# Parking the second experts' weights as plain values, and splitting them where they are used

## The chip, the cores and the metric

The kernel runs on one core of one Trainium2 chip. The metric is the device time of one execution in microseconds. The core's engines work side by side, each through its own instructions in order: TensorE (PE, with its weight loads as PEld), VectorE (DVE), ScalarE (ACT), GpSimd (POOL) and SyncE (SP), which here issues every DMA transfer.

## The reference

Three layers follow one another on 2304 tokens (4 batches of 576) and a model width of 512. All is float32; the expert weights arrive as float64.

```python
scores = scale * q @ k.T          # 4 batches, 8 heads, 576 x 576, head width 64
attn   = softmax(where(block_i >= block_j, scores, -1e9))   # blocks of 64
x  = (attn @ v)                   # heads joined: 2304 x 512
h  = max(x @ w1, x @ w2, x @ w3)  # first experts, width 768
x2 = h @ w_out                    # 2304 x 512
g  = 1 / (1 + exp(-(x2 @ w_gate)))  # second experts, width 1536
out = (g * (x2 @ w_val)) @ w_out2 # 2304 x 512
```

## The kernel before

**Arithmetic.** TensorE gets every float32 operand as two float32r parts: the high part is the value rounded by a copy (ScalarE or VectorE), the low part is the value less the high part (a subtraction on VectorE or GpSimd). A product is three matmuls: high by high, high by low, low by high. So each weight must be split once for each copy of it in SBUF.

**First stage, to about 551 us.** Attention for 32 jobs (batch, pair of heads, early or late rows) and the first experts for eight chunks of 256 or 320 tokens run interleaved. The work is a list of `Op`s with an engine (B means VectorE or ScalarE), a cost, dependencies, an earliest and a latest time and, for some, a ring of buffers. `plan()` is a list scheduler over these: it gives each engine's order, which TensorE, VectorE, ScalarE and SyncE then follow as written (`run_plan`). GpSimd's place is found by the framework's scheduler. The results x2 go out to DRAM (`x2d`).

In the same stretch the second experts' weights are parked in DRAM. The two halves of each of 12 block matrices (`park_pair`, from plan time 112 on, one every 20) are loaded as float64 words (`take`), turned into float32 in place (`first_part` on ScalarE, `shift` and `join` on VectorE), and combined into seven blocks of 128 x 256: three of the four quarters and four sums (a Strassen-Winograd scheme with seven products). `split_ops` splits each block: a high copy on VectorE or ScalarE, a low subtraction on GpSimd, and a store (L768) of both parts. The `sp` ring through which all this goes has two buffers. `park_out` does the same with the 12 output matrices, in two halves each. That makes 84 + 24 = 108 blocks.

**Second stage, from 551 us.** The tokens go in three chunks of 768. `take_x` loads a chunk of x2 and forms the seven combinations XC (four differences `t`, seven high copies on ScalarE, seven low subtractions on VectorE; L1062, L1066, L95). For each of 12 pairs `first`, `middle` and `last` run seven products of six matmuls of 384 columns (L1108 to L1110); VectorE adds their banks (L1121), ScalarE takes the sigmoid (L1133), VectorE multiplies (L1138), ScalarE and GpSimd split the hidden value (L1147, L95). The order of the products is first(n), last(n-1), middle(n). Then 12 x 6 output units (L1157 to L1159) use the output matrices. `take_w` loads one pair's seven split blocks, 1792 KB, into one of three buffers; `take_o` loads one split output matrix into one of four. In this stage only TensorE's order is written out; the framework's scheduler orders the other engines by the times given to `on` and its own estimate of when things are ready.

The stage's buffers lie where those of the first stage lay, so a write there waits for the last reader of the old tile. TensorE accumulates into eight banks, three to a pair.

Of the kernel before, what the change touches and what calls it, by code (L numbers as in the profile page):

```python
# [67 lines left out]
RING = {"qk": 2, "v": 3, "s": 3, "t": 2, "o": 1, "m": 2, "w": 8, "raw": 4, "tmp": 4, "st": 3, "sp": 2}  # L68
# [3 lines left out]
def block_attention_moe_moe(ctx: ExitStack, tc, k1, q1, v1, k2, q2, vt, wa, wb, out):  # L72
# [33 lines left out]
    sp_p = one.enter_context(tc.tile_pool(name="sp", bufs=RING["sp"]))  # L106
# [3 lines left out]
    pairs_d = [dram.tile([128, 7, 512], F32, name=f"pairs{n}") for n in range(NF2)]  # L110
    outs_d = [dram.tile([128, 2, PC], F32, name=f"outs{f}") for f in range(NF2)]
# [548 lines left out]
    def build():  # L660
# [57 lines left out]
        sums = []  # L718

        def word_ops(i, t):  # L720
# [17 lines left out]

            def join():
                lo, hi, _ = words()  # L740
                V.scalar_tensor_tensor(
                    out=hi, in0=hi, scalar=3, in1=lo, op0=ALU.logical_shift_left, op1=ALU.bitwise_or
                )

            ld = Op("S", 0.1, take, list(sums), ring="raw", size=512e3)
            new, last = [ld], [ld]
            if wide:
                p = Op(*act(PC), first_part, [ld])
                s = Op("V", 0.36, shift, [ld])
                last = [Op(*vec(PC), join, [p, s])]  # L750
                new += [p, s] + last
# [3 lines left out]
            return ld, last, lambda: words()[2] if wide else f32(box["x"])  # L755

        def split_ops(n, x, deps, dest, t):
            box = {}

            def high(e):  # L760
                box["t"] = sp_p.tile([128, 512], F32R, tag="sp", name="sp")[:, : 2 * n]
                copy(e, box["t"][:, :n], x())

            def low():
                sub("G", box["t"][:, n:], x(), f32(box["t"][:, :n]))

            def put():
                nc.sync.dma_start(out=dest, in_=f32(box["t"]))  # L768

            h = Op(*both(n, False), high, deps, ring="sp")  # L770
            l = Op("G", 0.2 + 0.0025 * n, low, [h])
            d = Op("S", 0.1, put, [l], size=1024 * n)
            h.frees = [d]
            for o in (h, l, d):
                o.early, o.late = t, t + P["slack"]
            return l

        def park_pair(n):
# [3 lines left out]
            la, da, xa = word_ops(3 * f + c, t)  # L782
            lb, db, xb = word_ops(3 * f + 3 + c, t)
# [508 lines left out]
```

## Time and profile before

| what | value |
|---|---|
| three timed runs | 980.91, 981.3, 984.16 us (median 981.3) |
| the profiled execution | 978.59 us, of which the span of the trace is 975.5 us |
| busy in the span | PE 910.8 us, DVE 596.8, ACT 418.7, POOL 166.4 |
| DMA | 146.80 MB read, 37.75 MB written |
| mean granted TensorE clock | 0.976 |

Busy time is read per engine: an engine that is busy for 93% of the span leaves 7% to be won by better feeding, unless its own work shrinks. A granted clock of 1.00 is 2.4 GHz, 0.50 is 1.2 GHz; a mean between them is a mixture. Idle time of an engine that nobody waits for costs nothing.

### The profile page before, as it was taken

How to read it: one execution, taken by the hardware profiler on the slowest of the kernel's cores; microseconds unless marked ns; L12 is line 12 of the kernel's file. 1: busy time of each engine (PE TensorE's matmuls, PEld its weight loads, DVE VectorE, ACT ScalarE, POOL GpSimd, SP SyncE). 2: the span in 40 equal slices, each digit the busy share in tenths (PEclk: the TensorE clock that was granted, in tenths of full speed). 3: DMA queues.
4: the chain of work that ended last, by engine and by line, in shares of the span. 5: the costliest groups of instructions: out<-in, count | busy, mean ns of one | idle time of the engine just before them, and what ended most of it. 6: DMA issues, size and time to landing. Idle time of an engine off the chain costs nothing.

```text
span 975.5 us, 15409 instructions
## 1 busy us (share of the span) xinstructions
PE 910.8 (93%) x5696; PEld 838.0 (86%) x5696; DVE 596.8 (61%) x1393; ACT 418.7 (43%) x1004; POOL 166.4 (17%) x186
## 2 busy tenths in 40 slices
PE   5598988998989999899999899999999999999998
PEld 4587988887878888789999899988899988999986
DVE  7999676878978959778842555570155550355500
ACT  6975443557655747467621323340133320333300
POOL 0000022212223222121200013230032320123300
PEclk9797999999999999999999999999999999999999
DMA  9911355655565664666335357775467663577233
GB/s 308 364 55 49 115 165 195 192 182 167 188 204 188 215 192 151 205 208 196 108 115 227 131 198 249 274 259 195 166 236 267 252 237 130 192 259 261 76 130 108
DMA packets 64763, 185.55 MB, mean 190 GB/s; under 512 B 8624, under 2 KB 25008, under 8 KB 60080
## 3 DMA queue, kind: packets, MB, share of 16 engines
q1 hardware_dynamic: 64688, 184.58, 55.3%
q8 instruction: 44, 0.72, 0.3%
q14 instruction: 31, 0.25, 0.1%
HBM read 146.80 MB, written 37.75 MB: 189 GB/s over the span
## 4 chain that ended last, share of the span: by engine, by line
PE 52%; DMA 4%; DVE 4%; issue 3%; POOL 1%; ACT 0%; SPq 0%; DVEq 0%; POOLq 0%; ACTq 0%
PE acc L1108 8%; PE acc L1109 8%; PE acc L1110 8%; PE acc L1157 5%; PE acc L1159 5%; PE acc L1158 5%; PE ps_m L527 2%; PE ps_m L525 2%; PE ps_m L526 2%; DMA pairs<-sp 2%; DVE xc L95 1%; PE ps_o L492 1%; PE ps_m L563 1%; PE ps_m L565 1%; PE ps_m L564 1%
## 5 line engine op out<-in xcount | busy, mean ns | idle before, releaser
L525 PE MATMUL ps_m<-XT,w 128*128 128x256 f32 (+1 forms) x576 | 179.4, 311 | 9.0 <-DVE m L536 3.7
L527 PE MATMUL ps_m<-XT,w 128*128 128x256 f32 (+1 forms) x576 | 173.4, 301 | 3.9 <-DVE w L95 3.9
L1108 PE MATMUL acc<-xc,wg 128*128 128x384 f32 x504 | 170.1, 338 | 4.3 <-DVE u L1121 2.9
L526 PE MATMUL ps_m<-XT,w 128*128 128x256 f32 (+1 forms) x576 | 173.2, 301 | 0.0
L1109 PE MATMUL acc<-xc,wg 128*128 128x384 f32 x504 | 169.5, 336 | 1.3 <-DVE xc L95 1.3
L1110 PE MATMUL acc<-xc,wg 128*128 128x384 f32 x504 | 169.6, 336 | 0.0
L525 PEld LDWEIGHTS ps_m<-XT,w 128*128 128x128 f32 x576 | 112.0, 194 | 13.7 <-DVE m L536 4.4
L527 PEld LDWEIGHTS ps_m<-XT,w 128*128 128x128 f32 x576 | 111.8, 194 | 4.5 <-DVE w L95 4.5
L526 PEld LDWEIGHTS ps_m<-XT,w 128*128 128x128 f32 x576 | 112.1, 195 | 0.7
L1108 PEld LDWEIGHTS acc<-xc,wg 128*128 128x128 f32 x504 | 95.4, 189 | 6.4 <-DVE u L1121 4.1
L95 POOL TENSOR_TENSOR sp<-praw,sp 128x256 fp32r<-128x256 f32 x60 | 49.0, 824 | 289.3 <-ACT sp L86 225.1
L1109 PEld LDWEIGHTS acc<-xc,wg 128*128 128x128 f32 x504 | 95.5, 189 | 1.7 <-DVE xc L95 1.6
L1110 PEld LDWEIGHTS acc<-xc,wg 128*128 128x128 f32 x504 | 95.3, 189 | 0.0
L400 ACT ACTIVATE E<-ps_s,nm 128x256 f32<-128x256 f32 (+3 forms) x128 | 66.4, 524 | 44.1 <-DVE nm L395 43.7
L1159 PE MATMUL acc<-ow,hid 128*128 128x512 f32 x216 | 84.2, 390 | 0.0
L1158 PE MATMUL acc<-ow,hid 128*128 128x512 f32 x216 | 84.1, 390 | 0.0
L1157 PE MATMUL acc<-ow,hid 128*128 128x512 f32 x216 | 84.0, 389 | 0.0
L90 DVE COPY osb<-acc 128x512 f32<-128x512 f32 x6 | 4.1, 692 | 118.5 <-PE acc L1159 110.8
L1121 DVE TENSOR_TENSOR u<-acc,p 128x384 f32<-128x384 f32 x72 | 40.1, 557 | 49.4 <-PE acc L1110 44.4
L1121 DVE TENSOR_TENSOR u<-acc,u 128x384 f32<-128x384 f32 x72 | 40.1, 556 | 46.3 <-PE acc L1110 45.1
L95 POOL TENSOR_TENSOR hid<-c,hid 128x384 fp32r<-128x384 f32 x18 | 19.1, 1061 | 286.8 <-ACT hid L1147 286.8
L492 PE MATMUL ps_o<-PT,v 128*64 128x320 f32 (+3 forms) x448 | 56.3, 377 | 10.4 <-DMA v<-in_v_dram 9.5
(109 smaller groups left out, 1815.4 us busy)
## 6 DMA issues: line engine op xcount, KB each, us to landing
wg<-pairs SPq DMA_DIRECT2D x36, 1792.0 KB, 7.4
pairs<-sp SPq DMA_DIRECT2D x84, 256.0 KB, 2.3
praw<-in_wb_dram SPq DMA_DIRECT2D x36, 512.0 KB, 4.5
ow<-outs SPq DMA_DIRECT2D x36, 512.0 KB, 3.3
qk<-in_k_dram SPq DMA_DIRECT2D x16, 576.0 KB, 4.3
wland<-in_wa_dram SPq DMA_DIRECT2D x5, 1536.0 KB, 17.4
outs<-sp SPq DMA_DIRECT2D x24, 256.0 KB, 2.5
v<-in_vt_dram SPq DMA_DIRECT2D x16, 320.0 KB, 3.4
```

Of the source, the lines that this page charges most:

```text
L95: (V if e == "V" else G).tensor_tensor(out=out, in0=a, in1=b, op=ALU.subtract)
L400: A.activation(E[h][:, e : e + 128 * (t + 1)], j.s[h, t], AF.Exp, bias=j.nm[:, c : c + 1], scale=1.0, accum_out=j.sm[:, c : c + 1],)
L525: T.matmul(ps, wt[:, 0, w, k], xh[:, k], start=(k == 0), stop=False)
L526: T.matmul(ps, wt[:, 0, w, k], xl[:, k], start=False, stop=False)
L527: T.matmul(ps, wt[:, 1, w, k], xh[:, k], start=False, stop=(k == KD - 1))
L1108: T.matmul(ps, w[:, 0, h], x[:, 0, h], start=start and h == 0, stop=False, skip_group_check=True)
L1109: T.matmul(ps, w[:, 0, h], x[:, 1, h], start=False, stop=False, skip_group_check=True)
L1110: T.matmul(ps, w[:, 1, h], x[:, 0, h], start=False, stop=h == 1, skip_group_check=True)
L1121: V.tensor_tensor(out=o, in0=BK[c, n, b][:, :N2], in1=x, op=ALU.add)
L1157: T.matmul(ps, h[:, 0, ct], w[:, 0], start=(f == 0), stop=False)
L1158: T.matmul(ps, h[:, 0, ct], w[:, 1], start=False, stop=False)
L1159: T.matmul(ps, h[:, 1, ct], w[:, 0], start=False, stop=(f == NF2 - 1))
```

## The change

The blocks and sums are parked as float32 values, unsplit. `join` writes its result into a new tile in block order (`blocks`, or `outw` for an output matrix) in place of the loaded words, so that a loaded tile comes free at once; the sums are formed from there, and four stores per pair and one per output matrix take the whole to DRAM (`put`), 60 in all in place of 108. `split_ops` and its `sp` ring are gone. The `raw` ring keeps its four buffers and now also carries `blocks` and `outw`; the ring of v goes from three to four.

In the second stage each pair's weights come as three parts: x (three blocks, used by `first`), z (two, `middle`) and y (two, `last`). For each part and chunk `take_w` loads the values into one of four `wr` buffers, copies the high part on ScalarE and subtracts the low part on VectorE (x, y) or GpSimd (z), into one of two buffers for each part. `take_o` does so with an output matrix (ScalarE and VectorE). The seven combinations, the temporaries and the other tiles of the stage are placed over other tiles of the first stage: the temporaries and XC[0] over the `raw` ring, the other six over the first three buffers of `w`. A sigmoid on a small tile is issued at TB - 24 on the plan's clock.

```diff
-RING = {"qk": 2, "v": 3, "s": 3, "t": 2, "o": 1, "m": 2, "w": 8, "raw": 4, "tmp": 4, "st": 3, "sp": 2}
+RING = {"qk": 2, "v": 4, "s": 3, "t": 2, "o": 1, "m": 2, "w": 8, "raw": 4, "tmp": 4, "st": 3}
...
-    sp_p = one.enter_context(tc.tile_pool(name="sp", bufs=RING["sp"]))
...
-    pairs_d = [dram.tile([128, 7, 512], F32, name=f"pairs{n}") for n in range(NF2)]
-    outs_d = [dram.tile([128, 2, PC], F32, name=f"outs{f}") for f in range(NF2)]
+    pairs_d = [dram.tile([128, 7, 256], F32, name=f"pairs{n}") for n in range(NF2)]
+    outs_d = [dram.tile([128, PC], F32, name=f"outs{f}") for f in range(NF2)]
...
-        def word_ops(i, t):
+        def word_ops(i, t, ring, dest, dring=None):
...
+            def two(x):
+                return x.rearrange("p (a n) -> p a n", a=2)
+
             def join():
+                o = dest()
+                if not wide:
+                    V.tensor_copy(o, two(f32(box["x"])))
+                    return
                 lo, hi, _ = words()
                 V.scalar_tensor_tensor(
+                    out=o.bitcast(U32), in0=two(hi), scalar=3, in1=two(lo),
+                    op0=ALU.logical_shift_left, op1=ALU.bitwise_or,
...
+            ld = Op("S", 0.1, take, ring, ring="raw", size=512e3)
...
+            j = Op("V", 0.72, join, deps, ring=dring)
+            new.append(j)
...
+            ld.frees = [j]
...
+        def put(out, src, deps, t):
+            d = Op("S", 0.1, lambda: nc.sync.dma_start(out=out, in_=src()), deps, size=512e3)
+            d.early, d.late = t, t + P["slack"]
+            return d
+
+        order_ = []
...
+            def corner(k):
+                def g():
+                    if "d" not in box:
+                        box["d"] = raw_p.tile([128, 4, 256], F32, tag="raw", name="blocks")
+                    return box["d"][:, ::3] if k == 0 else box["d"][:, 1:3]
+                return g
...
+            la, ja = word_ops(3 * f + c, t, list(order_), corner(0), "raw")
+            lb, jb = word_ops(3 * f + 3 + c, t, [la], corner(1))
+            order_[:] = [jb]
+            p = lambda f_, k: lambda: f_(k)
+            o1 = Op(*vec(256), two_of(ALU.add, p(s, 0), p(d, 1), p(d, 2)), [jb], ring="raw")
+            o2 = Op(*vec(256), two_of(ALU.subtract, p(s, 1), p(s, 0), p(d, 0)), [o1, ja])
+            o3 = Op(*vec(256), two_of(ALU.subtract, p(s, 2), p(d, 0), p(d, 1)), [o1, ja])
+            o4 = Op(*vec(256), two_of(ALU.subtract, p(d, 1), p(d, 3), p(s, 1)), [o2, o3])
...
+            order_[:] = [o1]
+            g = pairs_d[n]
+            w = [
+                put(g[:, 1:3], lambda: box["s"][:, 0:2], [o2], t),
+                put(g[:, 6], lambda: box["s"][:, 2], [o3], t),
+                put(g[:, 0], lambda: box["d"][:, 0], [ja], t),
+                put(g[:, 3:6], lambda: box["d"][:, 1:4], [o4], t),
+            ]
+            o1.frees = w[:2] + [o4]
+            ja.frees = w[2:]
...
+                box["d"] = raw_p.tile([128, PC], F32, tag="raw", name="outw")
+                return box["d"].rearrange("p (a n) -> p a n", a=2)
...
+            ld, j = word_ops(3 * f + 2, t, list(order_), dest, "raw")
+            order_[:] = [j]
+            j.frees = [put(outs_d[f], lambda: box["d"], [j], t)]
...
-    hid_p = pool("hid", 1)
-    xc_p = pool("xc", 1)
+    HID = []
+
+    def hidden(n):
+        p = pool(f"hid{len(HID)}", 1)
+        HID.extend(p.tile([128, 2, HC], F32R, name=f"hid{len(HID) + k}") for k in range(n))
+
+    XC = {}
+
+    def combos(ks):
+        p = pool(f"xc{len(XC)}", 1)
+        for k in ks:
+            XC[k] = p.tile([128, 2, 2, N2], F32R, name=f"xc{k}")
+
+    hidden(3)
+    ost_p = pool("ost", 3)
     tt_p = pool("tt", 2)
+    combos((0,))
+    hidden(2)
+    combos((4, 5, 1, 3, 2, 6))
     pt_p = pool("pt", 15)
-    hie_p = pool("hie", 1)
-    ost_p = pool("ost", 3)
+    hidden(7)
     ow_p = pool("ow", 4)
-    wg_p = pool("wg", 3)
+    wg_p = pool("wg", 2)
+    wr_p = pool("wr", 4)
     xr_p = pool("xr", 1)
+    warm = pool("warm", 1).tile([128, 8], F32, name="warm")
...
+    def take_w(c, n, part, t):
+        k0, k1, low = {"x": (0, 3, "V"), "y": (3, 5, "V"), "z": (5, 7, "G")}[part]
+        box = {}
+
+        def get():
+            box["r"] = wr_p.tile([128, 3, 256], F32, tag="wr", name="wr")[:, : k1 - k0]
+            nc.sync.dma_start(out=box["r"], in_=pairs_d[n][:, k0:k1])
+
+        def high():
+            WG[c, n, part] = wg_p.tile([128, 2, k1 - k0, 256], F32R, tag="wg" + part, name="wg" + part)
+            A.copy(WG[c, n, part][:, 0], box["r"])
+
+        def rest():
+            w = WG[c, n, part]
+            sub(low, w[:, 1], box["r"], f32(w[:, 0]))
+
+        on(t - 5.0, get)
+        on(t, high)
+        on(t + 0.7, rest)
...
+        def high():
             OW[c, f] = ow_p.tile([128, 2, PC], F32R, tag="ow", name="ow")
-            nc.sync.dma_start(out=f32(OW[c, f]), in_=outs_d[f])
-        on(t, g)
+            A.copy(OW[c, f][:, 0], box["r"])
+
...
+            part, i = (("x", 0), ("z", 0), ("y", 0), ("y", 1), ("x", 1), ("x", 2), ("z", 1))[k]
+            w = WG[c, n, part][:, :, i].rearrange("p s (k c) -> p s k c", k=2)
...
-    free_w = [TB - 22.0, TB - 15.0, TB - 8.0]
+    first_w = {"x": (18.0, 8.0), "y": (14.0, 4.0), "z": (16.0, 6.0)}
+
+    def next_w(c, n, part, t):
+        g = NF2 * c + n + 2
+        if g < NF2 * (TOK // HC):
+            take_w(g // NF2, g % NF2, part, t)
+
+    on(TB - 25.0, lambda: V.memset(warm, 0.0))
+    on(TB - 24.0, lambda: A.activation(warm, warm, AF.Sigmoid))
+    for n in range(2):
+        for part in "xzy":
+            take_w(0, n, part, TB - first_w[part][n])
     for c in range(TOK // HC):
...
-            take_w(c, n, free_w.pop(0))
...
+            next_w(c, n, "x", t)
...
+            next_w(c, n, "z", t)
...
+            next_w(c, n, "y", t)
...
-            if f >= 4:
-                take_o(c, f, t)
...
+            if f + 4 < NF2:
+                take_o(c, f + 4, t)
```

## Rows read from the trace of the kernel before

**Rows 1.** Windows: busy us (instructions) of PE, PEld, DVE, ACT, POOL; clock; DMA.

```profile
25.00:75.00 50.00, 38.21 (x268) 34.22 (x266) 47.95 (x125) 40.88 (x98) 0.00 (x0) 0.84 0.59 200
115.00:400.00 285.00, 258.97 (x1908) 234.29 (x1908) 229.19 (x606) 163.86 (x431) 67.41 (x84) 0.98 0.57 185
141.00:148.00 7.00, 6.13 (x36) 5.44 (x37) 6.29 (x17) 4.17 (x13) 0.51 (x2) 0.76 0.58 199
400.00:500.00 100.00, 98.67 (x693) 90.54 (x692) 82.38 (x212) 63.52 (x155) 18.67 (x24) 0.99 0.48 154
504.00:551.00 47.00, 47.00 (x321) 47.00 (x322) 13.73 (x27) 7.35 (x15) 0.00 (x0) 1.00 0.45 169
551.00:568.00 17.00, 12.63 (x54) 11.22 (x53) 12.14 (x17) 6.35 (x10) 0.00 (x0) 0.80 0.66 230
699.00:772.00 73.00, 73.00 (x423) 73.00 (x422) 37.65 (x68) 23.73 (x49) 19.16 (x18) 1.00 0.66 244
```

**Rows 2.** Who VectorE waited for, 115 to 500 us: total, times, longest.

```profile
DVE sp L90 <- DMA pairs<-sp: 27.0, 13, 5.6
```

**Rows 3.** The same for ScalarE, 115 to 500 us.

```profile
ACT sp L86 <- DMA pairs<-sp: 27.3, 17, 6.1
```

**Rows 4.** Timeline: VectorE's stalled casts and TensorE's gaps, first and last of nine.

```profile
139.54 0.71 DVE L90 CAST sp<-sums 128x256 fp32r<-128x256 f32 x1 [2.23 <-DMA pairs<-sp]
141.08 0.39 PE L563 MATMUL ps_m<-HR,w 128*128 128x256 f32 x1 [2.16 <-ACT HR L547]
...
395.63 0.29 DVE L90 CAST sp<-sums 128x256 fp32r<-128x256 f32 x1 [3.20 <-DMA pairs<-sp]
398.86 0.58 PE L378 MATMUL ps_s<-K,Q 128*128 128x512 f32 x1 [2.24 <-ACT E L436]
```

**Rows 5.** The tile sp: its high copies (ns min/median/max).

```profile
L86 ACT CAST sp<-praw x43: 413/424/442, 123.4 to 482.3; 128x256 fp32r<-128x256 f32 x43
L90 DVE CAST sp<-sums x28: 277/294/823, 135.8 to 396.3; 128x256 fp32r<-128x256 f32 x28
L90 DVE CAST sp<-praw x17: 277/291/667, 173.3 to 489.3; 128x256 fp32r<-128x256 f32 x17
```

**Rows 6.** Timeline of TensorE near the start of the kernel.

```profile
38.60 1.55 PE L492 MATMUL ps_o<-PT,v 128*64 128x256 f32 x8 [9.52 <-DMA v<-in_v_dram]
```

**Rows 7.** Timeline of the second stage's start: DVE, PE, ACT.

```profile
549.46 0.95 DVE L1062 TENSOR_TENSOR t<-xraw 128x768 f32<-128x768 f32 x1
551.49 0.34 PE L1108 MATMUL acc<-xc,wg 128*128 128x384 f32 x1
...
558.62 1.28 ACT L1133 ACT_TABLE_LOAD   x1
560.97 0.49 ACT L1133 ACTIVATE c<-acc 128x384 f32<-128x384 f32 x1 [1.07 <-PE acc L1110]
...
564.75 0.96 DVE L1062 TENSOR_TENSOR t<-xraw 128x768 f32<-128x768 f32 x1 [4.79 <-DMA xraw<-x2d]
565.78 0.34 PE L1110 MATMUL acc<-xc,wg 128*128 128x384 f32 x1
567.81 0.44 PE L1108 MATMUL acc<-xc,wg 128*128 128x384 f32 x1 [1.69 <-DVE u L1121]
568.10 0.34 PE L1109 MATMUL acc<-xc,wg 128*128 128x384 f32 x1
...
574.00 0.33 PE L1110 MATMUL acc<-xc,wg 128*128 128x384 f32 x1
```

**Rows 8.** The tile xc: high copies, low subtractions (ns min/median/max).

```profile
L1066 ACT CAST xc<-xraw x9: 826/837/837, 542.0 to 787.5; 128x768 fp32r<-128x768 f32 x9
L95 DVE TENSOR_TENSOR xc<-xraw,xc x9: 945/950/1762, 550.3 to 792.0; 128x768 fp32r<-128x768 f32 x9
```

**Rows 9.** The tile w, 25 to 60 us: subtractions of 512 columns.

```profile
L95 DVE TENSOR_TENSOR w<-wraw,w x6: 674/676/684, 30.4 to 50.4; 128x512 fp32r<-128x512 f32 x6
```

**Rows 10.** The tile u, 700 to 772 us: adds of a bank.

```profile
L1121 DVE TENSOR_TENSOR u<-acc,p x21: 557/557/558, 699.7 to 770.4; 128x384 f32<-128x384 f32 x21
```

More of the change, by code (lines that the diff above doesn't have):

```diff
@@ L716, in weights @@
             conv[i] = (h, l)
-        sums = []
-        def word_ops(i, t):
+        def word_ops(i, t, ring, dest, dring=None):
             box = {}
@@ L737, in shift @@
                 V.tensor_scalar(out=lo, in0=lo, scalar1=29, scalar2=None, op0=ALU.logical_shift_right)
+            def two(x):
+                return x.rearrange("p (a n) -> p a n", a=2)
             def join():
+                o = dest()
+                if not wide:
+                    V.tensor_copy(o, two(f32(box["x"])))
+                    return
                 lo, hi, _ = words()
                 V.scalar_tensor_tensor(
-                    out=hi, in0=hi, scalar=3, in1=lo, op0=ALU.logical_shift_left, op1=ALU.bitwise_or
-                )
-            ld = Op("S", 0.1, take, list(sums), ring="raw", size=512e3)
-            new, last = [ld], [ld]
+                    out=o.bitcast(U32), in0=two(hi), scalar=3, in1=two(lo),
+                    op0=ALU.logical_shift_left, op1=ALU.bitwise_or,
+                )
+            ld = Op("S", 0.1, take, ring, ring="raw", size=512e3)
+            new, deps = [ld], [ld]
             if wide:
@@ L749, in word_ops @@
                 s = Op("V", 0.36, shift, [ld])
-                last = [Op(*vec(PC), join, [p, s])]
-                new += [p, s] + last
+                deps = [p, s]
+                new += deps
+            j = Op("V", 0.72, join, deps, ring=dring)
+            new.append(j)
             for o in new:
@@ L754, in word_ops @@
             ld.early = t - P["load"]
[L755 to L776, printed above, removed]
+            ld.frees = [j]
+            return ld, j
+        def put(out, src, deps, t):
[3 more added lines that the diff above has]
+        order_ = []
         def park_pair(n):
@@ L781, in park_pair @@
             f, c = 2 * (n // 2), n % 2
-            la, da, xa = word_ops(3 * f + c, t)
-            lb, db, xb = word_ops(3 * f + 3 + c, t)
             box = {}
-            def blocks():
-                return xa()[:, :256], xa()[:, 256:], xb()[:, :256], xb()[:, 256:]
-            def s1():
-                box["s"] = raw_p.tile([128, 4, 256], F32, tag="raw", name="sums")
-                _, _, a21, a22 = blocks()
-                V.tensor_tensor(out=box["s"][:, 0], in0=a21, in1=a22, op=ALU.add)
@@ L806, in park_pair, with d, s @@
-            o3 = Op(*vec(256), s3, da + db)
-            o3.deps.append(o1)
-            o4 = Op(*vec(256), s4, [o2])
+            def corner(k):
[4 more added lines that the diff above has]
+                return g
+            def d(k):
+                return box["d"][:, k]
+            def s(k):
+                if "s" not in box:
+                    box["s"] = raw_p.tile([128, 4, 256], F32, tag="raw", name="sums")
+                return box["s"][:, k]
```

47 lines of the change are left out of this document (14 added, 33 removed).

## The prediction

> **What bounds the kernel now.** I read the windows first, stage by stage, then who waited for whom on VectorE and ScalarE, then TensorE's timeline with its gaps, last the tiles whose handling changes.
>
> The windows [rows 1] show TensorE as the bound wherever it is fed. From 699 to 772 us it is busy for all 73 us, from 504 to 551 for all 47, from 400 to 500 for 98.7 of 100. It is not fed in three places. At 25 to 75 us VectorE is the full engine, 47.95 of 50 us. At 115 to 400 TensorE is busy for 258.97 of 285 us, so 26.0 us idle, at a mean clock of 0.98. At 551 to 568 it is busy for 12.6 of 17 us at a clock of 0.80. No arithmetic of TensorE's changes, so what can be won lies in these places, and what can be lost lies in the second stage's products, where other engines get new work.
>
> Why is TensorE idle at 115 to 400? VectorE waits 27.0 us, in front of the high copies into sp, for stores from sp to land [rows 2], ScalarE another 27.3 us for the same [rows 3]. The ring has two buffers and seven blocks go through it in a row, each by copy, GpSimd, store. An engine that waits there holds up everything behind it: softmax maxima, evictions, splits. TensorE's timeline agrees. It has nine gaps above 1.5 us in the stretch, together 18.5 us, and each ends within five microseconds after such a stalled cast has run; the first and last stand in [rows 4]: casts held for 2.23 and 3.20 us, gaps of 2.16 and 2.24 us. Behind some of them the clock drops: 141 to 148 us runs at a mean of 0.76 [rows 1], which is 7 x 0.24 = 1.7 us of full-speed time lost. Four of the nine gaps are followed by such a stretch.
>
> **The parts and their costs.** The sum is made against the profiled execution, 978.6 us, of which the span is 975.5.
>
> *Parking, first stage.* Away go 108 high copies, 45 on VectorE at about 0.29 and 63 on ScalarE at about 0.42 us [rows 5], 13 and 26 us; 108 subtractions on GpSimd (67.4 + 18.7 = 86 us [rows 1]); 48 of 108 stores. The joins and sums stay, and only their destination changes. The stores left are issued by SyncE behind VectorE's join or sum in place of GpSimd's subtraction, so qk, v and word loads behind them on SyncE wait for a shorter chain. The stalls of [rows 2, 3] have no ring left to come from. I take the nine gaps, 18.5 us, as gone but for half a microsecond: **-18**. The ends are 0, if other waits fill the gaps, and -26, all idle time. For the clock I take three of the four drops, 3 x 1.7: **-5** (0 to -5.7, which is 2% of 285).
>
> *The ring of v.* TensorE waits 9.52 us for a v load that had to wait for a buffer [rows 6]. With a fourth buffer the load can go ahead of the weights. But VectorE is full at 25 to 75 us and works ahead on weight splits during that wait, so what is late next is VectorE. Only its 2 us of idle time there can come back: **-2** (0 to -9.5).
>
> *Tail of the first stage.* At 504 to 551 us TensorE is never idle, while VectorE has 33 and ScalarE 40 us free [rows 1]. Combinations and first weight splits can now move in there: 11 VectorE operations of 0.95 and seven ScalarE copies of 0.84 us [rows 8], plus two pairs' splits. Behind each on the same engine stands an eviction of a two-deep PSUM ring, so some matmul will wait: **+1** (0 to +4; 4 is a quarter of a microsecond at each of some 15).
>
> *Start of the second stage.* The first difference starts at 549.46 and the first product at 551.49, so products wait for combinations. Matmuls follow one another every (574.00 - 568.10) / 34 = 0.1735 us when fed. Up to the gap that ends at 567.81, eight products have run, 48 matmuls, 8.3 us of work in 16.3 us [rows 7]: 8.0 us lost, about 3 of them to the low clock [rows 1]. With temporaries and XC[0] on tiles that come free with the parking, and the rest on three weight tiles, the chain can run before 551. One stall may stay: VectorE waited 4.79 us for the next chunk's x, loaded and queued ahead of the adds [rows 7], and its order there is again the scheduler's estimate. I take **-6.5** (-3 to -8; -3 if half of the tiles come free only when the last projection ends).
>
> *The sigmoid's table.* The load takes 1.28 us, but the sigmoid behind it then waits 1.07 us for TensorE [rows 7]: covered now, so 0. If the products start without a stall, the early load keeps it from being exposed.
>
> *Products of the second stage.* A pair is 42 matmuls, 7.29 us, so 699 to 772 holds ten. VectorE works 3.75 us a pair, ScalarE 2.4, GpSimd 1.9 [rows 1]. New on VectorE are the low parts of x (768 columns, 0.95 us [rows 8]) and y (512, 0.68 [rows 9]): 5.4. ScalarE gets three copies, at most 0.84 each: below 4.9. GpSimd gets z, two blocks at 67.41 / 84 = 0.80 each: 3.5. None reaches 7.29, and a part has over a pair's time between its buffer coming free and its first use. The cost is in queueing. After the last matmul of product 6, two adds of 0.557 us [rows 10] must be through before product 2 writes that bank; in between TensorE has three products, 3.12 us. With about half a microsecond of hand-over the chain takes 1.6, so 1.5 us are left. A subtraction of 0.95 in front fits. One that meets GpSimd does not: the row shows up to 1.76 in place of 0.95 [rows 8]. That overruns by 0.26 us. At each of 36 pairs it would be 9 us, and I take a little under half: **+4** (0, if the queue is always clear, to +9; further out it is a rival).
>
> The Trainium skill (SBUF — State Buffer, "Who interferes with whom") says that a VectorE instruction with two SBUF inputs and a GpSimd instruction that reads SBUF exclude each other, and that the loser waits for the whole instruction. The slow 1.76 us subtraction agrees: 0.81 us lost to one neighbour. By that rule the new subtractions on VectorE compete with those on GpSimd, which speaks against this change; the rival below prices it.
>
> *Output units.* One split of 0.68 us on VectorE and one copy per four microseconds, hidden by engines that are nearly idle there; uncovered it would be 36 x 0.7 = 25 us, but four buffers keep it three matrices ahead. The halved traffic frees nothing that TensorE waited for: 0.
>
> The sum is -18 - 5 - 2 + 1 - 6.5 + 4 = -26.5, so 952.1 us by the profiled execution. The median of the timed runs is 981.3, 2.7 above that execution; I carry the same 2.7 over: **955 us**.
>
> **The rivals.**
>
> *The idle time returns elsewhere.* Blocks and sums share four buffers with the loaded words, and VectorE's join now waits for a buffer whose last store must land; everything behind it on VectorE waits too. For it: the same engine and the same kind of wait as in [rows 2]. Against it: two such waits a pair in place of seven, with a pair's 20 planned microseconds between, and a plan that counts the ring. Without the -18 and -5 the sum is -3.5, so 978; with half of them 966. I put this case at 970.
>
> *The combinations are late anyway.* If the weight tiles under XC come free only with the last projection, or the scheduler still queues the chain behind the last evictions, the start keeps most of its 8.0 us, and the new splits add to it: 961.
>
> *More is won.* All 26 us of idle time and 5.7 of clock, 4 at the start, 8 at the second stage's start, nothing lost in the products: -44, so 938 to 945.
>
> *The other side: VectorE falls behind in the products.* The place is the chain of two adds between product 6 and product 2. If GpSimd's 3.5 us a pair and VectorE's two-input SBUF work (0.95 + 0.68 + two multiplies of an add's size = 2.7) never overlap and the adds overlap neither, a pair takes 5.4 + 3.5 = 8.9 us on VectorE, 1.6 over TensorE's 7.29: 36 x 1.6 = 58 us, less the 30.5 won elsewhere, 1009. The point from which it loses anything is 1.9 us of mutual waiting a pair; from 0.85 us of stall a pair the change as a whole is a loss. Against it: the adds read PSUM, and in [rows 10] none is above 0.558 us while GpSimd works, so they can run beside it; even if GpSimd's 3.5 us exclude all 2.7, the two together are 6.2, still below 7.29. By the skill's rule taken whole, it is these 6.2 that count, and TensorE stays the bound.
>
> **How the numbers follow.** The forecast gets 0.60, the idle time's return 0.16 (three quarters of it faster), late combinations 0.09, more won 0.08, VectorE behind 0.07. About 0.3%, 3 us, is what a measurement can tell from no change. Faster: 0.60 + 0.12 + 0.09 + 0.08 = 0.89; same 0.04; slower 0.07. The range leaves out VectorE falling behind, the upper end of the returning idle time and the best end of more won: 940 to 973. The likeliest case alone, with its smaller terms at their ends, spans about 945 to 965.
>
> **What would show it.** Right: no sp rows, GpSimd idle until the second stage; TensorE idle under 10 us in the stretch that was 115 to 400 and no clock there below 0.95; combinations on VectorE well before the last projection ends and the first eight products in about 9 us; VectorE at 5.4 to 6.3 us a pair with TensorE full. Wrong: VectorE waits for stores into raw, in front of joins; TensorE gaps put down to u adds at every second pair; a second-stage start that still waits for xc.

## The result, and the profile after

| | median us | runs |
|---|---|---|
| before | 981.1 | 979.0 to 984.2 |
| after | 940.5 | 938.5 to 945.5 |

The ratio is 0.9591, with an interval of 0.9544 to 0.9638: 40.6 us faster. The forecast was 955, its range 940 to 973, and its sum -26.5. The profiled execution after has a span of 943.7 us, against 975.5.

The windows of the kernel after, in the stretches of [rows 1] (busy us and instructions of PE, PEld, DVE, ACT, POOL; clock; DMA):

```profile
25.00:75.00 50.00, 41.16 (x260) 34.48 (x259) 45.75 (x121) 39.38 (x96) 0.00 (x0) 0.84 0.61 208
115.00:400.00 285.00, 284.97 (x2179) 263.63 (x2179) 238.83 (x650) 167.55 (x430) 0.00 (x0) 1.00 0.51 164
400.00:500.00 100.00, 100.00 (x705) 94.20 (x705) 65.47 (x155) 49.70 (x111) 2.84 (x2) 1.00 0.39 125
504.00:551.00 47.00, 43.86 (x252) 43.00 (x251) 30.25 (x48) 21.86 (x38) 11.88 (x10) 0.96 0.37 114
699.00:772.00 73.00, 70.67 (x368) 66.31 (x367) 55.30 (x82) 39.68 (x73) 28.56 (x23) 0.98 0.39 119
```

From 115 to 400 us TensorE now idles for 0.03 us where it idled for 26.0, and the clock is 1.00 throughout; GpSimd has nothing to do. TensorE ran 2179 matmuls there in place of 1908 [rows 1]. These two windows do not hold quite the same work. The stretches from the first expert matmul of the second chunk to the second stage's first product do, 3066 matmuls each (windows of before and of after):

```profile
101.54:551.49 449.95, 422.59 (x3066) 388.04 (x3065) 334.49 (x869) 240.42 (x618) 86.08 (x108) 0.98 0.53 174
104.35:513.84 409.49, 409.46 (x3066) 381.87 (x3065) 314.49 (x831) 225.49 (x562) 2.84 (x2) 1.00 0.47 150
```

Of the 40.5 us between them 27.3 are idle time and 6.8 the clock (four times 3.4 us at 0.50 before, none after). The point on the first stage below comes back to what is left. The windows from 504 us on lie 38 us further into the program than in [rows 1], and those two are no longer full.

Whom TensorE waited for in the whole execution after (total, times, longest):

```profile
PE ps_s L377 <- DVE Q L358: 9.5, 4, 5.9
PE acc L1151 <- DVE u L1164: 8.7, 6, 2.0
PE ps_m L526 <- DVE w L95: 4.6, 5, 3.2
...
PE acc L1152 <- DVE xc L95: 1.5, 2, 1.1
```

The first and third lie before 104 us. The wait for v of [rows 6] is gone, and the waits for VectorE's Q have grown from 6.1 to 9.5 us (waits of TensorE before):

```profile
PE ps_s L378 <- DVE Q L359: 6.1, 2, 5.8
```

Those for u and xc are the second stage's.

Its start after, on the timelines of VectorE, ScalarE and TensorE, beside [rows 7]:

```profile
473.69 0.96 DVE L1078 TENSOR_TENSOR t<-xraw 128x768 f32<-128x768 f32 x1 [1.40 <-DMA xraw<-x2d]
...
475.96 0.95 DVE L95 TENSOR_TENSOR xc<-xraw,xc 128x768 fp32r<-128x768 f32 x1
...
514.04 0.49 DVE L90 COPY x2s<-ps_m 128x320 f32<-128x320 f32 x1 [2.15 <-PE ps_m L564]
514.45 1.82 DVE L95 TENSOR_TENSOR xc<-t,xc 128x768 fp32r<-128x768 f32 x2
...
504.37 1.56 ACT L1082 CAST xc<-t 128x768 fp32r<-128x768 f32 x2
...
516.32 0.44 PE L1152 MATMUL acc<-xc,wgx 128*128 128x384 f32 x1 [1.10 <-DVE xc L95]
...
521.22 0.41 PE L1151 MATMUL acc<-xc,wgz 128*128 128x384 f32 x1 [1.68 <-DVE u L1164]
```

The first difference starts 40 us before the first product (513.8) and two high parts follow at 504, but of the seven low parts only the first is early (475.96): the others come from 514.45 on, right behind the eviction of the last projection's bank at 514.04: in VectorE's order, not for want of data. TensorE runs into them at 516. The first eight products take 13.8 us, where they took 16.3 before.

Last, a place with no counterpart before, in the seventh and eighth pairs of each chunk (timelines of ScalarE, VectorE and TensorE after):

```profile
575.71 0.62 ACT L1130 CAST ow<-or 128x512 fp32r<-128x512 f32 x1 [3.61 <-DMA or<-outs]
...
576.37 0.69 DVE L95 TENSOR_TENSOR ow<-or,ow 128x512 fp32r<-128x512 f32 x1 [2.35 <-ACT ow L1130]
...
580.77 0.45 PE L1151 MATMUL acc<-xc,wgy 128*128 128x384 f32 x1 [1.96 <-DVE u L1164]
```

ScalarE stands 3.61 us for the load of an output matrix, VectorE 2.35 us behind ScalarE, and the additions behind both are late: TensorE waits 1.96 us. The same gap stands at 720.41 (1.95) and 861.38 (2.02), behind the same wait (timeline of ScalarE):

```profile
715.21 0.62 ACT L1130 CAST ow<-or 128x512 fp32r<-128x512 f32 x1 [3.34 <-DMA or<-outs]
...
856.32 0.62 ACT L1130 CAST ow<-or 128x512 fp32r<-128x512 f32 x1 [3.87 <-DMA or<-outs]
```

The load is late because its buffer is (timelines of GpSimd and SyncE):

```profile
571.26 1.75 POOL L95 TENSOR_TENSOR wgz<-wr,wgz 128x512 fp32r<-128x512 f32 x1
...
573.03 0.32 SPq L1126 DMA_DIRECT2D or<-outs  x1
```

SyncE issues it at 573.03, when GpSimd's subtraction of a pair's part z has given a buffer of the `wr` ring back, and ScalarE's cast follows at 575.71.

**Milestones.** The columns below are read from TensorE's timeline: where the second chunk of experts starts; the stretch from there to the first product of the second stage; the first 126 matmuls of the products, three pairs (fed: 21.9 us); what the next six pairs of the three chunks took above the 131.0 us they need when fed; the span. All are profiled executions.

| kernel | chunk 2 at | stretch | first three pairs | lost in later pairs | span |
|---|---|---|---|---|---|
| before | 101.5 | 450.0 | 30.0 | 0.0 | 975.5 |
| after | 104.4 | 409.5 | 27.4 | 8.4 | 943.7 |
| after, once more | 99.5 | 409.5 | 25.8 | 9.4 | 938.0 |
| store waits off, work kept | 99.3 | 412.9 | 25.8 | 9.0 | 941.1 |
| before, four sp buffers | 102.0 | 432.4 | 23.2 | 0.0 | 951.7 |
| old places | 101.6 | 409.5 | 32.2 | 10.2 | 947.2 |
| three v buffers | 100.7 | 409.8 | 25.8 | 8.4 | 938.6 |
| output splits spread | 103.6 | 409.5 | 25.8 | 0.0 | 932.4 |
| two low parts on GpSimd | 101.5 | 409.6 | 26.5 | 9.2 | 940.9 |
| no early table | 102.4 | 409.5 | 27.3 | 11.4 | 944.4 |
| low parts twice | 103.1 | 410.9 | 27.3 | 41.0 | 985.2 |
| own ring for output matrices | 101.2 | 409.6 | 27.3 | 0.0 | 931.6 |
| spread, and evictions moved | 99.6 | 409.7 | 23.9 | 0.0 | 926.9 |
| z on VectorE | 102.2 | 409.5 | 27.3 | 5.8 | 938.0 |

The difference of the two profiled spans, -31.8, is +2.9 - 40.5 - 2.6 + 8.4 by these columns. The first column scatters by 5 us between executions of the very same kernel (104.4 and 99.5); the stretch does not. That scatter goes with the granted clock: up to chunk 2 TensorE had 27.3 us at 0.50 in the one execution and 17.1 in the other, which makes 5.1 us of full speed. So a term before chunk 2 is known to a few microseconds, the stretch to tenths, the first three pairs to 1.6 us and the later pairs to 1. The medians give 40.6 us because the profiled execution after was the slowest of its four, and that of before was faster than all four of its timed runs; that it is the stretch's number too is chance.

### The profile page after: what moved, and what is told of

Its sections match the earlier page's. It is cut to its first block, busy times and chain, and to the rows that moved or that the text cites. A ratio compares the mean times of both kernels' runs of the same rounds, so it can differ in the third digit from the quotient of the medians.

```text
span 943.7 us, 15483 instructions
## 1 busy us (share of the span) xinstructions
PE 904.1 (96%) x5696; PEld 834.7 (88%) x5696; DVE 658.6 (70%) x1460; ACT 484.0 (51%) x1083; POOL 131.6 (14%) x114
## 5 line engine op out<-in xcount | busy, mean ns | idle before, releaser
L524 PE MATMUL ps_m<-XT,w 128*128 128x256 f32 (+1 forms) x576 | 176.1, 306 | 0.7 <-ACT w L710 0.6
L526 PE MATMUL ps_m<-XT,w 128*128 128x256 f32 (+1 forms) x576 | 172.0, 299 | 4.6 <-DVE w L95 4.6
L525 PE MATMUL ps_m<-XT,w 128*128 128x256 f32 (+1 forms) x576 | 171.4, 298 | 0.3 <-DVE XT L95 0.3
L95 POOL TENSOR_TENSOR wgz<-wr,wgz 128x512 fp32r<-128x512 f32 x36 | 52.5, 1458 | 649.9 <-ACT wgz L1111 649.9
L526 PEld LDWEIGHTS ps_m<-XT,w 128*128 128x128 f32 x576 | 110.0, 191 | 5.6 <-DVE w L95 5.6
L524 PEld LDWEIGHTS ps_m<-XT,w 128*128 128x128 f32 x576 | 110.1, 191 | 3.8 <-issue 1.4
L525 PEld LDWEIGHTS ps_m<-XT,w 128*128 128x128 f32 x576 | 110.3, 191 | 1.1 <-DVE XT L95 0.5
L1152 PE MATMUL acc<-xc,wgx 128*128 128x384 f32 x216 | 72.8, 337 | 1.1 <-DVE xc L95 1.1
L1151 PE MATMUL acc<-xc,wgx 128*128 128x384 f32 x216 | 72.7, 337 | 0.0
L1153 PE MATMUL acc<-xc,wgx 128*128 128x384 f32 x216 | 72.6, 336 | 0.0
L95 DVE TENSOR_TENSOR ow<-or,ow 128x512 fp32r<-128x512 f32 x36 | 31.0, 865 | 58.8 <-ACT ow L1130 58.7
L535 DVE TENSOR_TENSOR m<-ps_m,m 128x256 f32<-128x256 f32 (+1 forms) x96 | 43.6, 454 | 29.8 <-PE ps_m L526 28.0
L491 PE MATMUL ps_o<-PT,v 128*64 128x320 f32 (+3 forms) x448 | 58.5, 378 | 2.6 <-ACT PT L86 1.3
L1130 ACT CAST ow<-or 128x512 fp32r<-128x512 f32 x36 | 22.1, 621 | 74.7 <-PE acc L1202 58.2
L95 DVE TENSOR_TENSOR wgx<-wr,wgx 128x768 fp32r<-128x768 f32 x36 | 36.8, 1023 | 33.6 <-ACT wgx L1111 33.4
L562 PE MATMUL ps_m<-HR,w 128*128 128x256 f32 (+1 forms) x192 | 60.0, 313 | 0.3 <-ACT w L710 0.3
L563 PE MATMUL ps_m<-HR,w 128*128 128x256 f32 (+1 forms) x192 | 58.3, 304 | 1.0 <-DVE HR L95 1.0
L564 PE MATMUL ps_m<-HR,w 128*128 128x256 f32 (+1 forms) x192 | 58.4, 304 | 0.5 <-DVE w L95 0.5
```

The lines of the kernel that those rows point to most:

```text
L95: (V if e == "V" else G).tensor_tensor(out=out, in0=a, in1=b, op=ALU.subtract)
L524: T.matmul(ps, wt[:, 0, w, k], xh[:, k], start=(k == 0), stop=False)
L525: T.matmul(ps, wt[:, 0, w, k], xl[:, k], start=False, stop=False)
L526: T.matmul(ps, wt[:, 1, w, k], xh[:, k], start=False, stop=(k == KD - 1))
L562: T.matmul(ps, wh, hh, start=(f == 0), stop=False)
L1151: T.matmul(ps, w[:, 0, h], x[:, 0, h], start=start and h == 0, stop=False, skip_group_check=True)
```

## The experiments

The kernel before was timed beside each group (983.5, 984.5 and 985.3 us); ratios are to that.

**The kernel after once more**, unchanged, as a measure of scatter.

> The changed kernel once more, to see what repeats from execution to execution. From its first profile: the first matmul of the second chunk of experts at 104.4 us (before: 101.5), from there 409.4 us to the first product (before: 450.0), then 429.9 us to the end of the span (before: 424.0). If the 2.9 us lost ahead of 104 and the 2.3 to 3.8 us lost once in each chunk of products belong to the kernel, they come again within 1 us; if they belong to that execution, they don't. Ratio to before 0.955 to 0.964.

Measured: 940.4 us, ratio 0.956 (0.9529 to 0.9591). Stretch and later pairs repeat, 409.5 and 9.4; the first three pairs took 25.8 us, so differences of 1.6 us there mean nothing. Chunk 2 started at 99.5 us, so the 2.9 us lost ahead of it belong to that one execution.

**The stage-one work kept, the store waits off.** The 108 high copies and subtractions of parking run again in a two-buffer ring, but nothing is stored from it.

```diff
+            def high(e):
+                box["t"] = sp_p.tile([128, 512], F32R, tag="sp", name="sp")
+                copy(e, box["t"][:, :256], x())
+            def low():
+                sub("G", box["t"][:, 256:], x(), f32(box["t"][:, :256]))
...
+            h.frees = [l]
```

> The changed kernel, with the 108 high copies (VectorE or ScalarE) and 108 low subtractions (GpSimd) of the old parking put back into the first stage, into a ring of two that nothing stores from; their results are used by nobody. Theory: the first stage gained by the waits for stores that left the copies' ring, so work without those waits costs little: second chunk to first product 409 to 418 us, ratio 0.955 to 0.970. Rival: it gained by the work that left (VectorE 13, ScalarE 26, GpSimd 86 us): 435 to 450 us again, ratio 0.985 to 1.0.

Measured: 942.7 us, ratio 0.9589 (0.9553 to 0.9625). The work costs 3.4 us of the stretch (412.9 against 409.5), of some 40 that the change won. The window of that kernel:

```profile
115.00:400.00 285.00, 283.72 (x2148) 260.05 (x2147) 256.06 (x666) 188.51 (x490) 71.72 (x92) 1.00 0.52 165
```

GpSimd is as busy as before and VectorE busier (256.06 against 229.19), and TensorE is fed all the same. It was waiting, not work, that starved it.

**Before, with four sp buffers.** The other half: the stores stay, only the ring grows (room is made by cutting two other tiles to the size used).

```diff
-RING = {..., "st": 3, "sp": 2}
+RING = {..., "st": 3, "sp": 4}
```

> The kernel before, with four buffers in the ring sp in place of two (two rings of narrower tiles make the room: their tiles go from 512 and 384 to the 320 columns that are used). Theory of the waits: a cast now waits for the store of four casts ago, most stalls go, second chunk to first product falls from 450 to 420 to 435 us and the kernel to a ratio of 0.970 to 0.985. Rival of the work: nothing left, so within 0.3% of before.

Measured: 951.3 us, ratio 0.9665 (0.9625 to 0.9705). One number in the kernel before is worth 32 us. To the end of the last projection the stretch shrinks from 449.8 to 425.0 us, 25 of the 40. Waiting for stores is still there, 21.8 us in place of 54.3 [rows 2, 3]; how much of the other 15 us is due to it, no run separates (waits of VectorE and ScalarE in the kernel before with four buffers, 100 to 540 us):

```profile
DVE sp L90 <- DMA pairs<-sp: 14.0, 7, 3.4
...
ACT sp L86 <- DMA pairs<-sp: 7.8, 6, 3.1
```

Its second stage loses as much at its start as before, at another point: 7.4 us of waiting ahead of the first product and then 23.2 us for three pairs, together 30.6 against 30.0.

**The second stage's buffers in one block,** hidden values, combinations and temporaries in the order of the kernel before.

```diff
-    hidden(3)
-    ost_p = pool("ost", 3)
+    hidden(8)
+    combos((0, 1, 2, 3, 4, 5, 6))
     tt_p = pool("tt", 2)
-    combos((0,))
-    hidden(2)
-    combos((4, 5, 1, 3, 2, 6))
     pt_p = pool("pt", 15)
-    hidden(7)
+    hidden(4)
+    ost_p = pool("ost", 3)
```

> The changed kernel with the second stage's tiles in the old order (hidden values, all seven combinations, temporaries and so on, from the bottom). If the new places let the combinations start earlier, the first 126 products take more than the 27.4 us of the changed kernel, 30 or more as before (30.0), ratio to the changed kernel 1.002 to 1.006. Rival: the combinations' low parts stand behind the last evictions on VectorE in either case, and that sets the start: 27 to 28 us, no difference.

Measured: 949.0 us, ratio 0.9648 (0.9608 to 0.9689). The first three pairs take 32.2 us, so the new places are worth 4.8 to 6.4 us against the two runs of the kernel after. With the old places the start is 2.2 us worse than before the change, which is about what the new splits cost there, if it is more than scatter.

**Three v buffers.**

```diff
-RING = {"qk": 2, "v": 4, ...}
+RING = {"qk": 2, "v": 3, ...}
```

> The changed kernel with the ring of v back at three. Theory: the fourth buffer removes a 9.5 us wait of TensorE (first expert matmul at 32 in place of 40 us), but VectorE is the full engine there, so the second chunk of experts starts at about the same time: with three buffers 100 to 102 us, where the changed kernel had 99.5, 99.4, 101.6 and 104.4 in four profiles. Ratio to the changed kernel 0.998 to 1.003. Rival: the wait was worth most of its length, second chunk at 105 us or later and 4 to 8 us slower.

Measured: 940.3 us, ratio 0.9551 (0.9498 to 0.9603). TensorE's wait for v is back at 8.47 us (timeline of that kernel):

```profile
38.65 1.54 PE L491 MATMUL ps_o<-PT,v 128*64 128x256 f32 x8 [8.47 <-DMA v<-in_v_dram]
```

and chunk 2 starts at 100.7 us, inside the scatter of the kernels with four. The fourth buffer is worth nothing that can be measured.

**The output matrices' splits spread** over pairs three, five, seven and nine of a chunk.

```diff
-            if n == 6:
-                for f in range(4):
-                    take_o(c, f, t + f)
+            if n in (2, 4, 6, 8):
+                take_o(c, n // 2 - 1, t)
```

> The changed kernel with the first four output matrices of a chunk taken one at a time, after pairs 2, 4, 6 and 8, in place of all four after pair 6. Theory: the one slow spot in each chunk's products (pairs 6 to 8 take 24.1 to 25.6 us, the other groups of three 21.8) comes from VectorE and ScalarE standing in order behind output matrices whose loads have not landed; spread out, each group takes 21.8 to 22.5 us, and the kernel gains 6 to 9 us (ratio to before 0.947 to 0.950). Rival: it is VectorE's full load or its waits for GpSimd, and then the time only moves to other pairs: gain under 2 us.

Measured: 934.6 us, ratio 0.9472 (0.9406 to 0.9538). All that was lost in the later pairs is back, 8.4 to 0.0, and of TensorE's waits for u 2.4 us are left, at the stage's start (waits of that kernel):

```profile
PE acc L1151 <- DVE u L1164: 2.4, 3, 1.7
PE acc L1152 <- DVE xc L95: 1.4, 2, 1.1
```

**Two low parts of the first chunk's combinations on GpSimd.**

```diff
+            e = "G" if c == 0 and k in (4, 5) else "V"
-            return lambda: sub("V", XC[k][:, 1], x(), f32(XC[k][:, 0]))
+            return lambda: sub(e, XC[k][:, 1], x(), f32(XC[k][:, 0]))
```

> The changed kernel with the low parts of combinations 4 and 5 of the first chunk on GpSimd in place of VectorE, where they stand behind the last eviction. Theory: their place in VectorE's order is what delays the first products; the first 126 products fall from 25.7 to 27.4 us to 22 to 24, and the kernel gains 2 to 4 us. Rival: the chain behind them (the remaining differences, combinations 1, 3, 2 and 6, all on VectorE after the last eviction) takes over as the limit: gain under 1 us.

Measured: 942.6 us, ratio 0.9566 (0.9513 to 0.9618). They run early now (timeline of GpSimd in that kernel):

```profile
502.46 3.68 POOL L95 TENSOR_TENSOR xc<-t,xc 128x768 fp32r<-128x768 f32 x2 [20.28 <-ACT xc L1082]
```

so no buffer held them back, only VectorE's order; but the first three pairs stay at 26.5 us. The rest of the chain (a difference and four more low parts) still stands behind VectorE's last eviction and takes over.

**No early sigmoid table.**

```diff
-    on(TB - 25.0, lambda: V.memset(warm, 0.0))
-    on(TB - 24.0, lambda: A.activation(warm, warm, AF.Sigmoid))
```

> The changed kernel without the early sigmoid, so that the table is loaded in front of the first sigmoid of the second stage. Theory: 1.28 us on ScalarE with TensorE not waiting for that sigmoid directly: within 0.3% of the changed kernel, first 126 products within 1.3 us. Rival: ScalarE's queue is full just there, and the load is passed on: the start is 1.3 us longer or more.

Measured: 942.9 us (938.1 to 946.1), ratio 0.9567 (0.9507 to 0.9627). The load now lies in the stage's start (timeline of ScalarE):

```profile
518.69 1.28 ACT L1175 ACT_TABLE_LOAD   x1
519.99 0.49 ACT L1175 ACTIVATE c<-acc 128x384 f32<-128x384 f32 x1
```

and the first three pairs take 27.3 us, as in the kernel after. No difference that can be measured.

**The new low parts on VectorE done twice** (x and y, each written a second time with the same values): how near is the rival in which VectorE falls behind?

```diff
             sub(low, w[:, 1], box["r"], f32(w[:, 0]))
+            if part != "z":
+                sub(low, w[:, 1], box["r"], f32(w[:, 0]))
```

> The two low parts that VectorE computes for each pair in the second stage (0.95 and 0.69 us) are computed twice, the second time over the first with the same values, so VectorE has some 6.8 us of work in the 7.27 us that TensorE needs for a pair, against 5.15 of 7.27 in the changed kernel (15.48 us in a group of three pairs, 21.8 us). Theory of throughput: as long as VectorE's work fits into the pair, the products are fed; groups of three pairs stay at 21.8 us and the time within 3 us of the changed kernel's 940.5. Theory of the chain (the rival of the prediction in which VectorE falls behind): what counts is how late the two additions come between products 6 and 2, a subtraction more in front of them makes TensorE wait 0.5 to 1.5 us in most of the 36 pairs, and the time is 958 to 995 us, with waits of TensorE on u spread over all pairs.

Measured: 985.1 us (ten runs), ratio 0.9995 (0.9972 to 1.0017). The whole gain is gone: 41.0 us lost in six of twelve pairs of each chunk. It happens where the rival put it, though in 16 waits of up to 3.1 us and not in most of the 36 pairs. TensorE's waits in that kernel:

```profile
PE acc L1153 <- DVE u L1166: 39.0, 16, 3.1
```

One of the 16 on the timelines of VectorE, GpSimd and TensorE:

```profile
557.56 0.55 DVE L1166 TENSOR_TENSOR p<-acc,p 128x384 f32<-128x384 f32 x1
558.02 0.68 DVE L95 TENSOR_TENSOR wgy<-wr,wgy 128x512 fp32r<-128x512 f32 x1
558.62 1.37 DVE L1183 TENSOR_TENSOR p<-p,p 128x384 f32<-128x384 f32 x1
559.92 1.77 DVE L95 TENSOR_TENSOR wgy<-wr,wgy 128x512 fp32r<-128x512 f32 x1
561.61 1.01 DVE L1166 TENSOR_TENSOR u<-acc,p 128x384 f32<-128x384 f32 x2
...
558.26 1.32 POOL L95 TENSOR_TENSOR hid<-u,hid 128x384 fp32r<-128x384 f32 x1 [1.91 <-ACT hid L1192]
559.54 1.60 POOL L95 TENSOR_TENSOR wgz<-wr,wgz 128x512 fp32r<-128x512 f32 x1
...
563.14 0.44 PE L1153 MATMUL acc<-xc,wgy 128*128 128x384 f32 x1 [2.29 <-DVE u L1166]
```

But my arithmetic for it was wrong. Six pairs of VectorE's work in this kernel, from an addition to p to the same addition six pairs on:

```profile
557.56:612.95 55.39, 47.58 (x254) 46.62 (x253) 48.75 (x71) 28.34 (x52) 23.80 (x18) 0.94 0.37 119
```

The same six pairs of the kernel after:

```profile
551.98:598.25 46.27, 44.31 (x256) 43.97 (x255) 36.49 (x60) 27.89 (x53) 21.43 (x18) 1.00 0.47 142
```

VectorE has 48.75 / 6 = 8.1 us a pair, not 6.8. From 36.49 / 6 = 6.1 (5.15 where no output matrix is split) it rose by 2.0, though the added work is 1.64 when undisturbed. The other 0.4 us are instructions made longer: the multiply at 558.62 takes 1.37 us where it takes 0.55 alone, the subtraction at 559.92 takes 1.77 for 0.68, and both lie beside a GpSimd subtraction, while the additions that read PSUM keep their 0.55. At 8.1 of 7.28 us VectorE is simply over-full, so the run does not show that the chain alone decides. Over six pairs a pair took 9.2 to 9.8 us, more than VectorE's work by 1.1 or more; I put that down to the chain, which the run does not separate.

**A ring of their own for the output matrices.**

```diff
+    or_p = pool("or", 3)
...
-            box["r"] = wr_p.tile([128, 3, 256], F32, tag="wr", name="or")[:, :2].rearrange("p a n -> p (a n)")
+            box["r"] = or_p.tile([128, PC], F32, tag="or", name="or")
...
-                for f in range(4):
+                for f in range(3):
                     take_o(c, f, t + f)
+            if n == 8:
+                take_o(c, 3, t)
```

> The loads of the output matrices get a ring of three buffers of their own, and the first three of a chunk (fourth: two pairs later) are still split in one place in the seventh pair. Theory that the engines stand behind late loads (the 3.61 us wait of ScalarE for or and 2.35 us of VectorE behind it): the three loads no longer wait for buffers of the pairs' matrices, and the three long groups of pairs (24.1, 25.6, 24.2 us) fall to 21.8 to 22.3; the time is 933 to 936 us. Theory that the burst of splits itself is what makes the additions late: three of the four splits still come at once, so the groups stay at 23 us or more and the time at 938 us or more.

Measured: 935.0 us, ratio 0.9498 (0.9461 to 0.9535); nothing lost in the later pairs. That is what the theory of late loads wanted, but the run does not separate it from the burst: with loads free to go early the scheduler also moved the splits, to 512 us and to the end of the output units of the chunk before (the casts of the second chunk's stand at 641, 645 and 649 us). What speaks for the loads are the rows at 573 and 575 us above, with ScalarE and VectorE idle and not full in front of the gap in all three chunks, and that the kernel after had no tight burst either: its four casts stand at 566.84, 569.62, 571.48 and 575.71, the first and the last behind a load.

**Spread, and the last chunk's evictions on ScalarE.**

```diff
-        copy(e, s, pss[i, d])
+        copy("A" if i == 2 * B - 1 else e, s, pss[i, d])
```

> As the run with the output matrices' splits spread (934.6 us), and the last chunk's five results of the first stage are evicted by ScalarE in place of VectorE. Theory that the low parts at the second stage's start are late because they stand behind VectorE's last eviction: they now run before the last projection ends, TensorE's waits on xc and u between the first products go, the first 126 products take 22 to 23 us where the changed kernel needed 25.7 to 27.4, and the time falls by a further 3 us to about 931. Theory that the low parts are late for another reason (the buffers under them, or ScalarE, which now has evictions ahead of the casts): the first 126 products stay at 25 us or more and the time at 934 to 936.

Measured: 929.2 us (927.8 to 930.3), ratio 0.944 (0.9397 to 0.9482): the fastest version, 5% to 6% below before. (Its interval overlaps with that of the splits spread alone, so the further gain rests on the rows.) The first three pairs take 23.9 us, and TensorE's waits there are 2.1 us in place of 3.8 (waits of that kernel):

```profile
PE acc L1151 <- DVE u L1164: 1.4, 3, 0.6
PE acc L1152 <- DVE xc L95: 0.4, 1, 0.4
PE acc L1151 <- ACT p L1232: 0.3, 1, 0.3
```

The first low parts on its VectorE's timeline:

```profile
508.02 1.83 DVE L95 TENSOR_TENSOR xc<-t,xc 128x768 fp32r<-128x768 f32 x2 [7.60 <-ACT xc L1082]
```

The low parts start at 508.02, before the first product at 509.3 and not after it. Not earlier, since they now wait 7.60 us for ScalarE's casts, which have the evictions in front of them. So the first theory is shown, and part of the second holds too: 23.9 us lies between the two, and 2 us of the start are still lost.

**The third low part of each pair on VectorE.**

```diff
-        k0, k1, low = {"x": (0, 3, "V"), "y": (3, 5, "V"), "z": (5, 7, "G")}[part]
+        k0, k1, low = {"x": (0, 3, "V"), "y": (3, 5, "V"), "z": (5, 7, "V")}[part]
```

> The third low part of each pair moves from GpSimd to VectorE (0.69 us), so that GpSimd has only the low parts of the hidden values left: VectorE 5.8 us of 7.27 a pair, GpSimd some 35% less busy. Theory that the two engines hold each other up where both work on two inputs from SBUF: VectorE's long instances (a subtraction of 1.3 us where others take 0.55 to 0.69) become rarer and the products' groups shorten or stay; the time is 936 to 941 us. Theory that this costs nothing that TensorE sees: the groups of three pairs stay as they are and the time is 939 to 944 us, no faster.

Measured: 937.9 us, ratio 0.952 (0.9476 to 0.9563), overlapping with the kernel after run again (0.9529 to 0.9591). VectorE carries 38.86 / 6 = 6.5 us a pair, and TensorE is still fed except at the output matrices (window of six pairs):

```profile
539.00:583.80 44.80, 43.96 (x254) 43.64 (x253) 38.86 (x65) 27.74 (x53) 13.06 (x13) 1.00 0.50 149
```

No loss, and a gain that cannot be told from scatter: both theories stay possible. With the run in which the low parts are done twice, the point from which VectorE's work costs time lies between 6.5 and 8.1 us of it in a pair of 7.28.

## Why the prediction was right, and where it was not

The direction and the mechanism of the main term were right; the range held the time, by half a microsecond at its lower edge. That it did is in part luck: the first stage gave 18.5 us more than forecast, and the start and the products gave some 7 to 9 less. Step by step:

- **Parking and clock, -18 and -5: mis-sized.** The stretch, which holds the tail too, gave 40.5 us. The cause was as put: the two-buffer ring whose stores both engines waited for (four buffers alone return 25 us; the work alone costs 3.4). But the size was read from the nine gaps above 1.5 us, 18.5 us, and all 27.3 us of idle time in the stretch went; the clock gave 6.8. Even the two together, 34.1, are too small. What is left, 6.4 us, I put down to delays too short to show as idle time, as two fed matmuls on TensorE's timeline after show:

```profile
507.83 0.31 PE L563 MATMUL ps_m<-HR,w 128*128 128x320 f32 x1
507.97 0.31 PE L564 MATMUL ps_m<-HR,w 128*128 128x320 f32 x1
```

A matmul of 320 columns is drawn 0.31 us long and the next one starts 0.147 us later, so a matmul that comes up to 0.16 us late leaves no gap at all. The count of matmuls shows the same: 1908 where 2179 fit is 285 x (1 - 1908/2179) = 35.4 us of the window from 115 to 400 us, against 26.0 of idle time and 5.7 of clock (an approximate reading, as the two windows hold slightly different work).
- **Ring of v, -2 (0 to -9.5): about 0.** As said, VectorE is late next: the waits for its Q are 9.5 us with four buffers and 6.1 (before) or 5.5 (the run with three) without. That is some 4 of the 9.5 us; where the others went is not settled.
- **Tail, +1: 0.** The last chunk of the first stage took 42.2 us in both kernels.
- **Start of the second stage, -6.5: -2.6 to -4.2.** The new places gave 4.8 to 6.4 and the splits took some 2 back, if that is more than scatter. The first eight products took 13.8 and, in the other execution, 12.3 us; the prediction's sign of being right was about 9. What the prediction's rival on late combinations named, a chain queued behind the last evictions, is what kept the rest.
- **Sigmoid table, 0: right,** for the reason that other waits cover it even when it lies in the stage's start.
- **Products, +4 (0 to +9): +8.4 and +9.4, at the end of the bound and by another mechanism.** No loss came at "every second pair" from subtractions that meet GpSimd; VectorE's 5.15 us a pair, near the 5.4 worked out, left TensorE full in all other pairs. All of it came from the output matrices, which the prediction had costed at **0** as hidden. They share the four `wr` buffers with the pairs, so the last load of four comes late, and ScalarE and VectorE stand before it. This zero is the step that failed outright. (The half microsecond of hand-over in the chain of additions stands in no row. In the trace of before, additions from 700 to 772 us that VectorE had waited for started 0.04 to 0.14 us after the bank's last matmul, and TensorE 0.06 us after an addition that it had waited for.)

The rival "more is won", 938 to 945, has the number but not the account: it wanted 31.7 us of the first stage and nothing lost in the products, and got 40.5 and 8.4.

The rival on the other side, VectorE behind in the products, did not happen. The prediction allowed 1.9 us of mutual waiting a pair, which is 5.4 + 1.9 = 7.3 us of VectorE's time; the runs leave that point open, since 6.5 cost nothing and 8.1 the whole gain. Beyond it the loss is larger than VectorE's excess alone, which is all that the prediction's 1009 counted. On its mechanism the Trainium skill (SBUF — State Buffer, "Who interferes with whom") says that a VectorE instruction with two SBUF inputs and a GpSimd instruction that reads SBUF exclude each other. The rows at 558.62 and 559.92 agree: 0.82 and 1.09 us longer beside GpSimd. In the kernel after it happens too, and there TensorE does not feel it, since VectorE has room in a pair's 7.28 us (VectorE's groups from 510 us on: busy us, mean ns | idle before):

```profile
L1181 DVE TENSOR_TENSOR u<-u,u 128x384 f32<-128x384 f32 x36 | 26.6, 738 | 0.8
```

These multiplies take 0.55 us alone and 0.74 on average. With the output matrices' splits spread they still take 0.66 on average, and nothing is lost in the later pairs.

## What to carry to other kernels

Size what starves TensorE by its matmuls' pitch, counted instructions against those that would fit, and not by the large gaps: of 40.5 us here nine gaps held 18.5, all idle time 27, and some 6 left no gap at all. Before an operation is called hidden, ask what it waits for and what stands behind it in its engine's order: a 0.6 us copy that waits 3.6 us for a load from a shared ring cost more here (8.4 us in three chunks) than the start's share of all the splits that were moved (some 2). A chain that was placed early only starts early if no eviction stands in front of it on its engine, so move the evictions or the chain to another engine.

## What the runs showed of the hardware

- In the kernel with the low parts done twice, VectorE's multiplies of gate and value (128 x 384, two SBUF operands) that met a GpSimd subtraction took 1.2 us on average (31 of them, at most 1.37), the others 0.55 (23); its additions with one operand in PSUM took 0.55 us either way. Adding 1.64 us of two-operand SBUF work a pair cost VectorE 2.0.
- Two executions of one kernel differ by up to 5 us before the second chunk of experts and by less than 0.1 us in the 409.5 us behind it. The 5 us go with the granted clock: 27.3 us at 1.2 GHz in the one, 17.1 in the other.
